# Three real products in place of four for the complex matmul of a spectral layer, inside a fused one-core Trainium2 kernel

## The chip, the cores and the metric

The kernel runs on one core of a Trainium2 chip. The metric is the device time of one launch in microseconds, taken as the median of several runs. A core has TensorE (PE: matmuls, with a queue of its own for loading the stationary operand, PEld), VectorE (DVE), ScalarE (ACT), GpSimd (POOL) and SyncE (SP, which here only starts transfers). Each engine works through its own instructions in the order of the program. Matmul results land in PSUM, from where VectorE or ScalarE must fetch them; operands lie in SBUF.

## The reference

```python
X = np.fft.rfft(x, axis=1)                       # x: (8, 3008, 256)
Xr, Xi = X.real, X.imag
Yr = Xr @ w_r - Xi @ w_i + b_r                   # w: (256, 256)
Yi = Xr @ w_i + Xi @ w_r + b_i
Yr = np.sign(Yr) * np.maximum(np.abs(Yr) - 0.01, 0.0)     # the same for Yi
y = np.fft.irfft(Yr + 1j * Yi, n=3008, axis=1)
h = y.reshape(-1, 256) @ w_in                    # w_in: (256, 2048)
g = np.where(h > 0.0, h, np.exp(np.minimum(h, 0.0)) - 1.0)
out = g @ w_out                                  # w_out: (2048, 256)
```

So each batch passes a Fourier transform along its 3008 positions, a complex matmul over 256 channels with bias and soft threshold, the inverse transform, and then a two-layer network with ELU.

## The kernel before

The transform of length 3008 = 47 x 64 is done in steps of matmuls. For each batch there are units of five kinds, named by letters:

- **A** (6 units): the first transform step. Its result goes through DRAM and comes back in another order as the tile `Z`.
- **X** (8 units, `unit_X`): the second transform step, 8 small matmuls each. Its result is `XT`, in bfloat16, with 128 channels on the partitions, two halves of channels `dt`, a plane `c` for real and imaginary parts, and 1536 frequencies. ScalarE writes it from PSUM (line 128).
- **M** (12 groups, `unit_M(b, q, i)`, written M00 to M51 here): 128 frequencies each. `m_group` sums four matmuls of 512 columns, real plane with `wcat_r` = [w_r, w_i] and imaginary plane with `wcat_s` = [-w_i, w_r], for both `dt` (line 210). VectorE adds the bias out of PSUM into `yb` (line 220). GpSimd makes `clip` and subtracts it, which is the soft threshold, into `Y` (lines 231 and 232).
- **B** (6 units): the first inverse step, two M groups each, written by ScalarE as `Bz` (line 317); again through DRAM.
- **y** (8 units): the last inverse step, which writes `yT`, the input of the network.

The network works on blocks of 512 positions with 2048 hidden values, cut into 376 slots of 256 hidden values. `front(i)` computes `hps` (line 933) in PSUM and ScalarE takes the exponential. `elu` clips it and `finish_elu` forms `gT`: on VectorE line 988 and line 977 as a rule; in a slot that holds an M group ScalarE does two steps (lines 951 and 952) and VectorE line 975 only; in a slot without any unit GpSimd clips (line 986). `back(i)` multiplies `gT` with `w_out` into `ps_o` (line 1007) two slots later, and every eighth slot `osb` is copied out (line 1019).

The order is written out by hand. While the network of batch b runs, the units of batch b+1 are put into its 47 slots by `plan(b)`, one unit a slot, in the order y, X0 to X7, M00 M01 M10 M11 B0 M20 M21 B1 and so on to B5, then A of the batch after, with the y units 6 and 7 between. In a slot the unit comes first, then the matmuls of `front`, then `gT` of the slot before, then `elu`, then the matmuls of `back`. The input transfers are started by GpSimd in three slots of a batch.

Three PSUM pools matter. All units share one tile of two banks (`psF`). `hps` has two tiles (`psH`), so the matmuls of a slot wait until `gT` of two slots earlier has read its tile. `ps_o` has two.

Batch 0 is done ahead of the network with functions of its own (`first_M`, `last_M`, which stand on `m_group` or repeat its four products); the change leaves them as they are. `last_M` (line 276) has matmuls of 256 columns.

Of the kernel before, what the change touches and what calls it, by code (L numbers as in the profile page):

```python
# [8 lines left out]
ALU = mybir.AluOpType  # L9
AF = mybir.ActivationFunctionType  # L10
BF16 = mybir.dt.bfloat16
F32 = mybir.dt.float32
# [17 lines left out]
def kernel(  # L30
# [11 lines left out]
    nc = tc.nc  # L42
    P = nc.NUM_PARTITIONS

    B, S, D = x.shape
# [5 lines left out]
    LAM = 0.01  # L51
# [9 lines left out]
    wcat_r = constp.tile([P, 2, 2 * D], BF16, name="wcat_r")  # L61
    wcat_s = constp.tile([P, 2, 2 * D], BF16, name="wcat_s")
    w_in_s = constp.tile([P, 2, DFF], BF16, name="w_in_s")
    w_out_r = constp.tile([P, NFT, E], F32R, name="w_out_r")
    bias_bc = constp.tile([P, 2 * D], F32, name="bias_bc")
# [15 lines left out]
    wk2 = ctx.enter_context(tc.tile_pool(name="wk2", bufs=2))  # L81
    wk3 = ctx.enter_context(tc.tile_pool(name="wk3", bufs=3))
# [20 lines left out]
    XT_of = {}  # L103
    Y_of = {}
# [14 lines left out]
    def unit_ps(name, alone):  # L119
        if alone:  # L120
            return pre2.tile([P, 2, 512], F32, name=name, tag="pre2")
        return psF.tile([P, 2, 512], F32, name=name, tag="fps")

    def evac(dst, src, on_dve):
        if on_dve:
            nc.vector.tensor_copy(dst, src)
        else:
            nc.scalar.copy(dst, src)  # L128
# [45 lines left out]
        q.dma_start(Z_of[b][r0:r1, s0:s1, :], dv[r0:r1, s0:s1, :])  # L174

    def unit_X(b, u, alone=False, on_dve=False, apart=False):
        g, dt = u // 2, u % 2
        if u == 0:
            XT_of[b] = xtp.tile([P, 2, 2, K1 * N2], BF16, name="XT", tag="XT")
        XT, Z = XT_of[b], Z_of[b]  # L180
        if apart:
            psv = [t[:].rearrange("p (k j) -> p k j", j=P) for t in two_banks(pre1, "mps1")]
        else:
            ps = unit_ps("xps", alone)
            psv = [ps[:].rearrange("p a (k j) -> p (a k) j", j=P)]
        nk = 8 // len(psv)
        for kk in range(8):
            k = 8 * g + kk
            nc.tensor.matmul(  # L189
                psv[kk // nk][:, kk % nk, 0 : 4 * K1], lhsT=Z[:, k, dt * P : dt * P + P],  # L190
                rhs=M2[:, k].rearrange("p c m -> p (c m)"), start=True, stop=True,
            )
        for h, v in enumerate(psv):
            k0 = 8 * g + nk * h
            evac(
                XT[:, dt].rearrange("p c (m s) -> p c m s", s=NS)[:, :, :, k0 : k0 + nk],
                v[:, :, 0 : 4 * K1].rearrange("p k (c m) -> p c m k", c=2),
                bool(h) if apart else on_dve,
            )

    mps_of = {}

    def m_group(b, q, i, ps, biased=False):
        XT = XT_of[b]
        o = (2 * q + i) * P
        todo = [(c, dt) for c in range(2) for dt in range(2)]
        if b == 0:
            todo.sort(key=lambda z: z[1])
        for c, dt in todo:
            nc.tensor.matmul(  # L210
                ps, lhsT=XT[:, dt, c, o : o + P], rhs=(wcat_r, wcat_s)[c][:, dt, :],
                start=(not biased and (c, dt) == (0, 0)), stop=((c, dt) == (1, 1)),
            )
        if i == 0:
            Y_of[b, q] = wk3.tile([P, 2, 2 * D], BF16, name="Y", tag="Y")
        if biased:
            yb = ps
        else:
            yb = wk3.tile([P, 2 * D], F32, name="yb", tag="yb")[:]
            nc.vector.tensor_tensor(yb, ps, bias_bc[:], ALU.add)  # L220
        if (b, q, i) == (0, 2, 0):
            clip = late3.tile([P, 2 * D], F32, name="gT", tag="gT")
        else:
            clip = wk2.tile([P, 2 * D], F32, name="clip", tag="clip")
        return yb, clip

    def unit_M(b, q, i):
        if i == 0:
            mps_of[b, q] = unit_ps("mps", False)
        yb, clip = m_group(b, q, i, mps_of[b, q][:, i, :])  # L230
        nc.gpsimd.tensor_scalar(clip[:], yb, LAM, -LAM, ALU.min, ALU.max)  # L231
        nc.gpsimd.tensor_tensor(Y_of[b, q][:, i, :], yb, clip[:], ALU.subtract)  # L232

    held = []

# [104 lines left out]
    def two_banks(pool, n):  # L340
        return [pool.tile([P, 512], F32, name=n, tag=n) for _ in range(2)]
# [133 lines left out]
    busy = constp.tile([P, 512], BF16, name="busy")  # L475
# [279 lines left out]
    gatep = ctx.enter_context(tc.tile_pool(name="gatep", bufs=2))  # L755
    late2 = ctx.enter_context(tc.tile_pool(name="late2", bufs=2))
    late3 = ctx.enter_context(tc.tile_pool(name="late3", bufs=3))

    w_in_v = moe_w_in.rearrange("(c p) f -> p c f", p=P)
    w_out_v = moe_w_out.rearrange("(t p) e -> p t e", p=P).bitcast(F32R)  # L760
# [23 lines left out]
    def gate(src):  # L784

        t = gatep.tile([P, 1], F32, name="gate", tag="gate")
        nc.gpsimd.tensor_copy(t[0 : src.shape[0], :], src)
# [15 lines left out]
    for u in range(8):  # L803
        unit_X(0, u, alone=True, on_dve=u == 1, apart=u > 3)
        if u == 1:
            nc.vector.tensor_tensor(w3[:], v3[:], w3[:], ALU.subtract)
        if u < 4:
            idle_pe(1)
# [88 lines left out]
    FILL = 10  # L897
# [136 lines left out]
    def put(kind, b, *a):  # L1034
        return ({"A": unit_A, "X": unit_X, "M": unit_M, "B": unit_B, "Y": unit_Y}[kind], (b, *a))

    def plan(b):

        f0 = [[] for _ in range(PER)]
        f1 = [[] for _ in range(PER)]  # L1040
        n1, n2 = b + 1, b + 2
        mid = [("X", u) for u in range(8)] + [
            ("M", 0, 0), ("M", 0, 1), ("M", 1, 0), ("M", 1, 1), ("B", 0), ("M", 2, 0),
            ("M", 2, 1), ("B", 1), ("M", 3, 0), ("M", 3, 1), ("B", 2), ("M", 4, 0),
            ("M", 4, 1), ("B", 3), ("M", 5, 0), ("M", 5, 1), ("B", 4),
            ("A", 0), ("B", 5), ("A", 1), ("A", 2), ("A", 3), ("A", 4),
        ]
        if n1 < B:
            lead, seq = 0, [("y", u) for u in range(2, 6)] + mid
            if b:  # L1050
                seq.insert(20, ("y", 6))
                seq.insert(24, ("y", 7))
                xs = (3, 8, 13)
                seq += [("A", 5)] * (5 if n2 == B else 1) + [("n", 0), ("n", 1)]
            else:
                lead, seq = FILL, (
                    [u for u in mid if u[0] != "A"]
                    + [("A", 0), ("A", 1), ("A", 2), ("n", 0), ("n", 1)]
                    + [("A", u) for u in range(3, 6)]
                )  # L1060
                xs = (12, 15, 18)
        else:
            lead, seq = 0, [("y", u) for u in range(2, 8)]
        for t, u in enumerate(seq, lead):
            if u[0] == "y":
                f0[t].append(put("Y", b, u[1]))
            elif u[0] == "n":
                f0[t].append(put("Y", n1, u[1]))
            elif u[0] == "A":
                if n2 < B:  # L1070
                    f0[t].append(put("A", n2, u[1]))
            else:
                f0[t].append(put(u[0], n1, *u[1:]))
            if u == (("A", 1) if b and n2 < B else ("B", 5)):
                f1[t] += [
                    (load_Bs, (n1, w, 0, 4 * K1 - 16 * (b == w == 0))) for w in range(4)
                ]
            if u == ("A", 5) and n2 < B:
                f1[t] += [(load_Z, (n2, s0, s1)) for s0, s1 in ((0, 8), (8, NS))]
        if b == 0:  # L1080
            for t in range(6):
                f1[t].append((unit_A, (1, t, False, t not in (0, 2), True)))
            for t, a, u in (
                (7, f0, 2), (7, f1, 3), (8, f0, 4), (8, f1, 5), (9, f0, 6), (9, f1, 7)
            ):
                a[t].append((split_Y, (0, u)))
            f1[1].insert(0, (scale_w_in, (1, True, 1)))
            for w in range(1, 4):
                f1[w].append((load_Bs, (0, w)))
            f1[5] += [(load_Z, (1, s0, s1)) for s0, s1 in ((0, 8), (8, 16), (16, NS))]  # L1090
            f1[xs[0]].append((lambda: gate(Z_of[1][:, 16, 0:1]), ()))
        if n2 < B:
            for ci in range(3):
                f1[xs[ci]].append((load_x, (n2, ci)))
        return f0, f1
# [4 lines left out]
    for i in range(n + LAG):  # L1100
        if i == FILL:
# [4 lines left out]
                        name=n_, bufs=k_, space=bass.MemoryType.PSUM, reuse_waits="tile"  # L1106
# [8 lines left out]
        elif i < n:  # L1115
            r = i % PER
            if r == 0:
                f0, f1 = plan(i // PER)
# [58 lines left out]
```

## Time and profile before

| what | value |
|---|---|
| median of 3 runs | 904.38 us (903.83 to 907.98) |
| the profiled execution | 903.61 us, span 901.8 us |
| granted TensorE clock | 0.998 |
| TensorE busy | 883.2 us (98%) |
| VectorE, ScalarE, GpSimd busy | 717.0, 696.8 and 325.5 us (80%, 77%, 36%) |
| line 210, the M groups' matmuls of 512 columns in `mps` | 342 recorded, 106.5 us busy |
| line 232, GpSimd's subtract | 84, 1276 ns each |
| line 231, GpSimd's clip | 84, 614 ns each |
| line 988, VectorE's clip of the exponential | 190, 692 ns each |

Busy time is the union of an engine's instructions. TensorE's instructions overlap each other in a pipeline, so the length of a matmul in the profile (379 ns for 512 columns) is longer than its pace, which is read from the starts of neighbours. Times in the timeline are microseconds from the start of the span; a bracket at the end of a line is the idle time before it and what ended it.

### The profile page before, as it was taken

Reading aid. Unit: us, or ns where it says so; the run is one execution under the profiler, and the core shown is the slowest. Engines: PE = TensorE matmul, PEld = TensorE weight load, DVE = VectorE, ACT = ScalarE, POOL = GpSimd, SP = SyncE. Lnnn points to the kernel's source line nnn. Section 1 sums busy time; section 2 is a strip of 40 time slices with the busy share of each in tenths; the row PEclk is TensorE's granted clock in tenths of the full one; section 3 lists DMA queues with packets and bytes.
Section 4 is the critical chain, followed back from the end, with each engine's and each line's share of the span. In section 5 each row is a group of like instructions: output and inputs, shape, how many; then the busy total and the mean of one; then the engine's idle time right before and its main releaser. Section 6 shows DMA issues by size and latency. Waiting matters only on the chain.

```text
span 901.8 us, 17335 instructions
## 1 busy us (share of the span) xinstructions
PE 883.2 (98%) x6670; PEld 653.2 (72%) x6773; DVE 717.0 (80%) x907; ACT 696.8 (77%) x876; POOL 325.5 (36%) x464
## 2 busy tenths in 40 slices
PE   8899999999999999999999999999999999999997
PEld 3467667876688667876678766787667866777776
DVE  8788768877788778897788877888778877778776
ACT  6778788877878778788887888878887877777664
POOL 7561540144230531405504153133332134443664
PEclk9999999999999999999999999999999999999999
DMA  8996226621473226713266041752228111231011
GB/s 265 308 259 188 90 68 183 199 71 48 129 200 118 71 64 163 207 60 94 59 199 187 25 110 55 213 161 81 61 73 231 28 42 50 71 96 48 24 48 48
DMA packets 90489, 105.80 MB, mean 117 GB/s; under 512 B 5363, under 2 KB 81142, under 8 KB 86982
## 3 DMA queue, kind: packets, MB, share of 16 engines
q1 hardware_dynamic: 84054, 76.64, 30.3%
q0 software_dynamic: 5968, 27.26, 9.2%
q8 instruction: 53, 0.87, 0.4%
q10 hardware_dynamic: 384, 0.79, 0.3%
q14 instruction: 30, 0.25, 0.1%
HBM read 54.86 MB, written 49.81 MB: 116 GB/s over the span
## 4 chain that ended last, share of the span: by engine, by line
PE 87%; DVE 4%; ACT 4%; issue 2%; DMA 2%; POOL 1%; DVEq 0%; SPq 0%; ACTq 0%; POOLq 0%
PE ps_o L1007 35%; PE hps L933 34%; PE mps L210 8%; PE yps L467 2%; PE bps L304 2%; PE aps L152 2%; PE xps L189 2%; DVE gT L977 1%; DVE Et L988 1%; ACT Et L954 1%; DMA xt<-in_x_dram 1%; ACT Et L951 1%; ACT Bz L317 1%; DMA Z<-DA 1%; PE sps L933 1%
## 5 line engine op out<-in xcount | busy, mean ns | idle before, releaser
L1007 PE MATMUL ps_o<-w_out_r,gT 128*128 128x256 f32 x3008 | 475.4, 301 | 0.0
L1007 PEld LDWEIGHTS ps_o<-w_out_r,gT 128*128 128x128 f32 x3008 | 403.1, 189 | 48.5 <-DVE osb L1019 1.3
L933 PE MATMUL hps<-yT,w_in_s 128*128 128x512 bf16 (+7 forms) x1613 | 372.0, 350 | 5.1
L975 DVE SCALAR_TENSOR_TENSOR gT<-Et,hps 128x512 fp32r<-128x512 f32 (+1 forms) x268 | 220.2, 851 | 73.3 <-POOL Et L986 37.0
L977 DVE SCALAR_TENSOR_TENSOR gT<-hps,Et 128x1024 fp32r<-128x1024 f32 x190 | 232.4, 1223 | 16.0 <-PE hps L933 1.4
L933 PEld LDWEIGHTS <-w_in_s 128*128 128x128 bf16 x1728 | 141.6, 98 | 128.6 <-issue 21.4
L986 POOL TENSOR_SCALAR Et<-Et 128x512 f32<-128x512 f32 x204 | 121.5, 614 | 226.8 <-ACT Et L949 217.1
L954 ACT ACTIVATE Et<-hps 128x1024 f32<-128x1024 f32 x190 | 195.7, 1030 | 9.1 <-PE hps L933 3.0
L988 DVE TENSOR_SCALAR Et<-Et 128x1024 f32<-128x1024 f32 x190 | 131.4, 692 | 44.4 <-ACT Et L954 37.4
L231 POOL TENSOR_SCALAR clip<-yb 128x512 f32<-128x512 f32 x84 | 51.6, 614 | 315.5 <-DVE yb L220 278.0
L949 ACT ACTIVATE Et<-hps 128x512 f32<-128x512 f32 x182 | 98.8, 595 | 61.9 <-PE hps L933 60.5
L951 ACT ACTIVATE Et<-hps 128x1024 f32<-128x1024 f32 x84 | 86.2, 1026 | 71.7 <-PE hps L933 70.2
L232 POOL TENSOR_TENSOR Y<-yb,clip 128x512 bf16<-128x512 f32 x84 | 107.2, 1276 | 7.0
L952 ACT ACTIVATE Et<-Et 128x1024 f32<-128x1024 f32 x84 | 88.8, 1058 | 2.7
L220 DVE TENSOR_TENSOR yb<-mps,bias_bc 128x512 f32<-128x512 f32 x88 | 60.5, 689 | 35.6 <-PE mps L210 23.4
L128 ACT CAST XT<-xps 128x768 bf16<-128x768 f32 x59 | 47.0, 799 | 14.9 <-PE xps L189 14.8
L210 PE MATMUL mps<-wcat_s,XT 128*128 128x512 bf16 x173 | 53.3, 379 | 0.8 <-issue 0.2
L210 PE MATMUL mps<-wcat_r,XT 128*128 128x512 bf16 x169 | 53.2, 384 | 0.3 <-ACT Bz L317 0.3
L128 ACT CAST A<-aps 128x1024 bf16<-128x1024 f32 x42 | 42.5, 1014 | 13.9 <-PE aps L152 12.6
L128 ACT CAST yT<-yps 128x752 bf16<-128x752 f32 x56 | 44.1, 788 | 9.2 <-PE yps L467 9.1
L210 PEld LDWEIGHTS <-XT 128*128 128x128 bf16 x380 | 30.3, 98 | 28.8 <-issue 0.9
L317 ACT CAST Bz<-bps 128x1024 bf16<-128x1024 f32 x42 | 42.0, 1000 | 1.7 <-PE bps L304 1.7
(166 smaller groups left out, 475.7 us busy)
## 6 DMA issues: line engine op xcount, KB each, us to landing
xt<-in_x_dram POOLq DMA_DIRECT2D x21, 1024.0 KB, 6.4
out_dram<-osb SPq DMA_DIRECT2D x158, 128.0 KB
Bs<-DB SPq DMA_DIRECT2D x30, 384.0 KB
DB<-Bz SPq DMA_DIRECT2D x20, 512.0 KB
DA<-A SPq DMA_DIRECT2D x19, 512.0 KB
Z<-DA SPq DMA_DIRECT2D x6, 1152.0 KB
xt<-in_x_dram POOLq DMA_DIRECT2D x6, 512.0 KB, 6.2
Z<-DA SPq DMA_DIRECT2D x8, 384.0 KB
```

Source lines behind the costliest of these rows:

```text
L128: nc.scalar.copy(dst, src)
L210: nc.tensor.matmul(ps, lhsT=XT[:, dt, c, o : o + P], rhs=(wcat_r, wcat_s)[c][:, dt, :], start=(not biased and (c, dt) == (0, 0)), stop=((c ...
L232: nc.gpsimd.tensor_tensor(Y_of[b, q][:, i, :], yb, clip[:], ALU.subtract)
L933: nc.tensor.matmul(hps[s][:, c0:c1] if early else hps[:, s, c0:c1], lhsT=w_in_s[:, dt, ft * P : ft * P + P], rhs=yT_of[b][:, dt, t0 : t0 + ...
L949: nc.scalar.activation(E_[:, s], hps[:, s], AF.Exp)
L951: nc.scalar.activation(E_, hps[:], AF.Relu, scale=-1.0)
L954: nc.scalar.activation(E_, hps[:], AF.Exp)
L975: nc.vector.scalar_tensor_tensor(o, e, -1.0, h, ALU.add, ALU.max)
L977: nc.vector.scalar_tensor_tensor(o, h, 0.0, e, ALU.max, ALU.add)
L986: nc.gpsimd.tensor_scalar(E_[s], E_[s], 1.0, 0.0, ALU.min, ALU.max)
L988: nc.vector.tensor_scalar(E_, E_, 1.0, -1.0, ALU.min, ALU.add)
L1007: nc.tensor.matmul(po[q][:, i_ % 2, :], lhsT=gT[:, s, i_ * P : i_ * P + P], rhs=w_out_r[:, ft, :], start=(ft == 0 and i_ % 2 == 0), stop=( ...
```

## The change

For batches 1 to 7 an M group is formed by three real products:

- shared = (Xr + Xi) w_r
- Yr = shared + Xi (-w_i - w_r)
- Yi = shared + Xr (w_i - w_r)

The sums of weights are made once, in place in `wcat_s`, by two GpSimd steps after batch 0 (`three_weights`). The plane Xr + Xi is made per batch by six adds of 128x512 (`sum_XT`): five on GpSimd, of which three behind X3 and two behind X7, and one on VectorE just ahead of M00. For this X is done for the first 128 channels in units 0 to 3 and for the others in units 4 to 7. An M group is then six matmuls of 256 columns, each group in a `psF` tile of its own. VectorE copies the shared product out of PSUM into one half of `yb`, then adds it to both other products. GpSimd adds the bias ahead of its clip and subtract.

```diff
     def unit_X(b, u, alone=False, on_dve=False, apart=False):
-        g, dt = u // 2, u % 2
+        g, dt = (u % 4, u // 4) if b else (u // 2, u % 2)
...
+        if b and u % 4 == 3:
+            for ch in range(dt, 3):
+                sum_XT(b, dt, ch, nc.gpsimd)
+
+    def sum_XT(b, dt, ch, eng):
+        XT, m = XT_of[b], slice(512 * ch, 512 * ch + 512)
+        eng.tensor_tensor(sum_of(dt, ch), XT[:, dt, 0, m], XT[:, dt, 1, m], ALU.add)
+
+    def sum_of(dt, ch):
+        return XS[:, 3 * dt + ch] if 3 * dt + ch < 5 else busy[:]
+
+    def three_weights():
+        r, s = wcat_r, wcat_s
+        nc.gpsimd.tensor_tensor(s[:, :, 0:D], s[:, :, 0:D], r[:, :, 0:D], ALU.subtract)
+        nc.gpsimd.tensor_tensor(
+            s[:, :, D : 2 * D], r[:, :, D : 2 * D], s[:, :, D : 2 * D], ALU.subtract
+        )
...
     def unit_M(b, q, i):
+        XT, o = XT_of[b], (2 * q + i) * P
+        if (q, i) == (0, 0):
+            sum_XT(b, 1, 0, nc.vector)
         if i == 0:
-            mps_of[b, q] = unit_ps("mps", False)
-        yb, clip = m_group(b, q, i, mps_of[b, q][:, i, :])
-        nc.gpsimd.tensor_scalar(clip[:], yb, LAM, -LAM, ALU.min, ALU.max)
-        nc.gpsimd.tensor_tensor(Y_of[b, q][:, i, :], yb, clip[:], ALU.subtract)
+            Y_of[b, q] = wk3.tile([P, 2, 2 * D], BF16, name="Y", tag="Y")
+        ps = unit_ps("mps", False)
+        ch, oc = divmod(o, 512)
+        r, s = wcat_r, wcat_s
+        for out_, lhs, w in (
+            (ps[:, 1, 0:D], None, r[:, :, 0:D]),
+            (ps[:, 0, 0:D], XT[:, :, 1, o : o + P], s[:, :, 0:D]),
+            (ps[:, 0, D : 2 * D], XT[:, :, 0, o : o + P], s[:, :, D : 2 * D]),
+        ):
+            for dt in range(2):
+                nc.tensor.matmul(
+                    out_, lhsT=lhs[:, dt] if lhs is not None else sum_of(dt, ch)[:, oc : oc + P],
+                    rhs=w[:, dt, :], start=(dt == 0), stop=(dt == 1),
+                )
+        yb = wk3.tile([P, 2 * D], F32, name="yb", tag="yb")
+        clip = wk2.tile([P, 2 * D], F32, name="clip", tag="clip")
+        evac(yb[:, D : 2 * D], ps[:, 1, 0:D], True)
+        nc.vector.tensor_tensor(
+            yb[:].rearrange("p (c d) -> p c d", c=2),
+            ps[:, 0].rearrange("p (c d) -> p c d", c=2),
+            yb[:, D : 2 * D].unsqueeze(1).to_broadcast([P, 2, D]), ALU.add,
+        )
+        nc.gpsimd.tensor_tensor(yb[:], yb[:], bias_bc[:], ALU.add)
+        nc.gpsimd.tensor_scalar(clip[:], yb[:], LAM, -LAM, ALU.min, ALU.max)
+        nc.gpsimd.tensor_tensor(Y_of[b, q][:, i, :], yb[:], clip[:], ALU.subtract)
...
+            f1[FILL + 2].append((three_weights, ()))
```

## The prediction

> **What bounds the kernel now.** I read the page's first lines, then the groups by shape, then the timeline engine by engine through one round of M and B groups, and last the timeline of the start, where VectorE and GpSimd touch each other. The page first:
>
> ```profile
> PE 883.2 (98%) x6670; PEld 653.2 (72%) x6773; DVE 717.0 (80%) x907; ACT 696.8 (77%) x876; POOL 325.5 (36%) x464
> ...
> PE 87%; DVE 4%; ACT 4%; issue 2%; DMA 2%; POOL 1%; DVEq 0%; SPq 0%; ACTq 0%; POOLq 0%
> ```
>
> TensorE is busy for 98% of the span and carries 87% of the chain that ended last. Fewer TensorE cycles should therefore pay, unless something else was only just in time. The timeline around groups B0, M20 and M21 of one batch shows how close that is. Columns are start, length, engine, line:
>
> ```profile
> 199.62 0.61 PE L210 MATMUL mps<-wcat_r,XT 128*128 128x512 bf16 x2
> ...
> 200.49 1.03 PE L933 MATMUL hps<-yT,w_in_s 128*128 128x512 bf16 x4
> ...
> 202.30 0.61 PE L210 MATMUL mps<-wcat_r,XT 128*128 128x512 bf16 x2
> ...
> 203.17 1.03 PE L933 MATMUL hps<-yT,w_in_s 128*128 128x512 bf16 x4
> ...
> 200.43 0.69 DVE L988 TENSOR_SCALAR Et<-Et 128x1024 f32<-128x1024 f32 x1 [0.60 <-ACT Et L954]
> 201.04 0.68 DVE L220 TENSOR_TENSOR yb<-mps,bias_bc 128x512 f32<-128x512 f32 x1
> 201.64 1.22 DVE L977 SCALAR_TENSOR_TENSOR gT<-hps,Et 128x1024 fp32r<-128x1024 f32 x1
> 203.45 0.69 DVE L220 TENSOR_TENSOR yb<-mps,bias_bc 128x512 f32<-128x512 f32 x1 [0.59 <-PE mps L210]
> ```
>
> The hps matmuls at 203.17 reuse the bank pair that gT of 201.64 reads until 202.86. So TensorE got the bank 0.31 us before it needed it, and VectorE (L988, yb, gT without a gap) is what fills it. In the X slots the margin is 0.17 us (gT 172.57 to 173.79, hps 173.96). TensorE is the bound with VectorE 0.2 to 0.3 us behind it.
>
> **TensorE's gain.** An M group takes from 199.62 to 200.49, 0.87 us for four matmuls of 512 columns. Matmuls of 256 columns on the same tiles stand at line 276: their five run from 43.04 to 43.60, 0.112 us each, so six take 0.67. The gain is 0.20 us a group, 84 x 0.20 = 16.8 us if TensorE stays the bound.
>
> **VectorE's additions.** yb (0.60 us to the next start) becomes a copy of 256 columns and an add of 512. The add is priced at L220. The copy has its own row, 420 ns:
>
> ```profile
> L232 POOL TENSOR_TENSOR Y<-yb,clip 128x512 bf16<-128x512 f32 x84 | 107.2, 1276 | 7.0
> ...
> L1022 DVE COPY osb<-ps_o 128x256 f32<-128x256 f32 x2 | 0.8, 420 | 0.8 <-PE ps_o L1007 0.8
> ```
>
> The add reads what the copy wrote. L988 followed by its gT shows that cost: 0.10 us after the end (208.70 + 0.69, then 209.49) where independent steps start 0.08 before it. So the pair adds 0.42 + 0.10 = 0.52 us. In the changed program only the last of the six matmuls of a group signals, and the copy waits for that one, so nothing of it is hidden under the group.
>
> M following M: from the group's start the matmuls end at 0.67, VectorE starts 0.28 later (before: 202.30 + 0.87, start 203.45), copy to 1.37, add from 1.47, gT from 2.07 to 3.29, bank free about 3.35. TensorE wants it at 2.48 + 0.67 = 3.15. It waits 0.20, and the slot stays at its 2.68 us. The three groups M01, M10, M11 gain nothing.
>
> Pairs behind a B or y slot (M20/M21 to M50/M51, four a batch): here L988 of the slot before comes late, VectorE is 0.52 longer, TensorE 2 x 0.20 earlier, and the margin was 0.31, about 0.25 after signalling. TensorE waits 0.52 + 0.40 - 0.25 = 0.67, less 0.40 gained: +0.27 a pair. Where the slot before is a y slot the margin was 0.56 (gT 221.65 to 222.87, hps 223.43), so about +0.02.
>
> **GpSimd's additions.** Each M group now has the bias add besides clip and subtract. A two-input add of 128x512 is 1.28 us (L232), clip 0.70 to the next start: 1.37 + 0.70 + 1.37 = 3.4 us a group. M, M, B takes about 7.7 us and brings 6.9 us of that, so GpSimd works nearly without pause from M00 to the last B. What this does to L988 is to be read at the start of the run, where the same kind of VectorE instruction (two SBUF sides, float32 in) meets GpSimd:
>
> ```profile
> 38.02 1.24 DVE L779 TENSOR_SCALAR w_in_s<-w_in_f 128x512 bf16<-128x512 f32 x1
> ...
> 52.87 0.42 DVE L779 TENSOR_SCALAR w_in_s<-w_in_f 128x512 bf16<-128x512 f32 x1
> ...
> 37.71 1.27 POOL L261 TENSOR_TENSOR Y<-yb,clip 128x512 bf16<-128x512 f32 x1
> ```
>
> Alone it takes 0.42. Begun under GpSimd's subtract, which ends at 38.98, it ends at 39.26, 0.28 after it: it was held until GpSimd was through. Of the 190 L988 none overlaps a GpSimd computation in the trace of before; gT and yb, which read PSUM, overlap many and keep their length. So only L988 is exposed. Met at random by a back-to-back GpSimd, it waits (1.28² + 1.28² + 0.61²) / (2 x 3.4) = 0.54 us on average and then saves 0.14 of its start: +0.39. Bounds are 0 and 1.28. That goes straight into the wait of a pair: 0.27 + 0.39 = 0.66 behind a B, 0.41 behind a y, so 2 x 0.66 + 2 x 0.41 = 2.1 us a batch.
>
> **The plane sums.** Three on GpSimd after X3, two after X7, and one on VectorE ahead of M00. I price those on GpSimd at 1.28 (bounds 0.61, the one-input row, and 1.5, the longest row of a 512 step, L714). Count from an X slot's start by the slot at 180.05: XT is written at 1.35 (181.40), L988 due 2.48 to 3.17. The sums run 1.44 to 2.72, then L988 first (it ends 3.27, GpSimd's next is held to it), 3.27 to 4.41, 4.50 to 5.78. L988 of X4, due at 4.63, is held to 5.78 and ends 6.33 in place of 5.32. One us less the margin: +0.9 a batch.
>
> M00: VectorE's sum stands in its queue behind L988 of X7, which waits for ScalarE's exp and for GpSimd's first sum; it ends at 3.27. The sum itself has no row; bounds by line 650 (96x384, 0.56) and line 806 (128x768, 0.95), I take 0.64. It ends at 3.83, TensorE at 2.15 + 0.11 = 2.26 has nothing else in its queue: a wait of 1.63, less 0.20 gained, +1.43. The page VectorE: DVE Perf Modes of the Trainium skill (the perf-mode tier table) puts a bfloat16 add from SBUF at two elements a cycle, an estimate of 0.42 here and 1.5 us less over the run; no row shows one.
>
> Nothing is moved past a queue that matters: the input DMAs of GpSimd come up to 4 us later, tens of us before their use. X1 and X2 of batch 1 read later parts of Z than before; the last part had landed by 76.40, X2 starts at 76.60. The two steps on the weights (2.6 us, once) lie beside X. B4 and B5 wait for GpSimd's last subtract, most where B5 follows B4 at once: 0 to 1 us a batch, I take 0.5.
>
> **The sum.** A batch: 0.9 + 1.43 + 0 + 2.1 + 0.5 = 4.9 us, times 7 = 34.5. The profiled execution took 903.61 (span 901.8), which gives 938.1; the median of the runs shown is 0.8 above it: 939.
>
> A rule that speaks harder against the change: the Trainium skill, SBUF — State Buffer, Who interferes with whom, has a VectorE step with two SBUF inputs blocked by a GpSimd step that reads SBUF. The row nearest is line 654, two such inputs, at 21.79: 0.60 us, no longer than its sisters, though GpSimd's L714 had begun at 21.23. So I let the DVE sum go ahead; by the rule it waits for GpSimd's second sum (see the third rival).
>
> **Rivals.**
> One, L988 isn't held: the four lines above are then four of the start only. X costs nothing, pairs 2 x 0.27 + 2 x 0.02 = 0.6, M00 3.73 - 2.26 - 0.20 = 1.3: with the B groups 0.3, 2.2 a batch, 15 in all: 919. Against it: all L779 begun under GpSimd end 0.28 after it. Chance 0.16.
>
> Two, the waits are absorbed and TensorE's gain stays, ending faster: 904 - 16.8 = 888. It decides itself at hps: VectorE's pair would have to cost under 0.10 us more than yb, not 0.52, and the M00 sum be there 1.6 us earlier. Nothing in the profile has such a cover. Chance 0.05. If only M00's wait is absorbed and L988 isn't held, the batch costs 2.2 - 1.6 = 0.6: 908, no change to be measured, chance 0.04.
>
> Three, VectorE's M00 sum is held too, by the second GpSimd sum (3.27 to 4.41), ending at 4.91: 1.1 us more a batch, 947; with GpSimd's adds at 1.5 some 953. Chance 0.2.
>
> Four, the change doesn't save TensorE time: 256 columns at line 1007's pace (1.27 us for eight, 0.158) make a group of 0.95. M00 to M11 each get 0.28 longer than I forecast, 4 x 0.28 x 7 = 8: 947. Against it stands line 276. Chance 0.04.
>
> **Numbers.** My forecast has 0.51. Eight in ten: from 917, just under the first rival, to 953. Faster by over 0.5% (4.5 us, about what a measurement of this kernel tells from no change) 0.05, within 0.04, slower 0.91.
>
> **What would show it.** Right: L988 in M and X slots longer than 0.70 with ends 0.55 behind GpSimd's; TensorE idle about 1.6 us before M00, released by DVE; idle before hps released by gT; GpSimd over 55% busy. Wrong: L988 at 0.69 beside GpSimd (first rival), or TensorE waiting for none of them and M groups of 0.67 (second).

## The result, and the profile after

The changed kernel takes 940.27 us (median of 6 runs, 938.56 to 941.77); the kernel before took 903.98 us in the same session (903.69 to 907.98). The ratio is 1.0393, with a 95% interval of 1.0373 to 1.0413: slower by 36 us. The profiled execution took 940.29 us, its span is 938.5 us and its granted clock 0.993. The forecast was 939, in a range of 917 to 953.

First the page of the changed kernel: busy times, chain, and four groups (line, engine, operation, count, then busy us, mean ns of one, and the idle time before them):

```profile
PE 883.3 (94%) x6838; PEld 673.5 (72%) x6941; DVE 776.1 (83%) x998; ACT 697.5 (74%) x876; POOL 482.3 (51%) x585
...
PE 59%; DVE 20%; ACT 11%; issue 6%; DMA 2%; POOL 1%; DVEq 0%; SPq 0%; ACTq 0%; POOLq 0%
...
L1033 DVE TENSOR_SCALAR Et<-Et 128x1024 f32<-128x1024 f32 x190 | 151.1, 795 | 44.2 <-ACT Et L999 37.7
...
L273 POOL TENSOR_TENSOR yb<-yb,bias_bc 128x512 f32<-128x512 f32 x84 | 107.6, 1281 | 78.9 <-DVE yb L268 78.7
...
L207 POOL TENSOR_TENSOR XS<-XT 128x512 bf16<-128x512 bf16 x28 | 35.2, 1272 | 126.3 <-ACT XT L128 126.3
...
L261 PE MATMUL mps<-wcat_r,XS 128*128 128x256 bf16 x140 | 31.5, 283 | 19.5 <-DVE XS L207 15.0
```

TensorE fell from 98% busy to 94%, and of the chain that ended last it now carries 59% in place of 87%; VectorE has taken 20%. Line 1033 is line 988 of before, the clip of the exponential: its mean went from 692 to 795 ns, 19.7 us more over 190 of them. The waits of TensorE name what ends them (us in total, times, longest):

```profile
PE hps L978 <- DVE gT L1022: 15.2, 46, 0.9
PE mps L261 <- DVE XS L207: 15.0, 7, 2.2
PE mps L261 <- DVE yb L268: 3.9, 12, 0.5
```

To see where the time went I laid the slots of the two traces beside each other, each from the start of its `ps_o` to that of the next. The spans differ by 36.7 us:

| slots (sum over 7 batches) | forecast | measured |
|---|---|---|
| X0 to X7 | +6.3 | +4.0 |
| M00 and M01 | +10.0 | +18.3 (17.2 and 1.1) |
| M10, M11 | 0 | -1.8 |
| the four pairs M20/M21 to M50/M51 | +14.7 | +12.5 |
| B0 to B5 | +3.5 | +4.2 (B5 2.0, B0 1.2) |
| all others | 0 | -0.4 |

**An X slot.** The timeline (start, length, engine, line) through the first three sums of the batch that follows the stretch shown of before:

```profile
187.37 1.23 DVE L1033 TENSOR_SCALAR Et<-Et 128x1024 f32<-128x1024 f32 x1
188.70 1.23 DVE L1022 SCALAR_TENSOR_TENSOR gT<-hps,Et 128x1024 fp32r<-128x1024 f32 x1
...
184.19 3.86 POOL L207 TENSOR_TENSOR XS<-XT 128x512 bf16<-128x512 bf16 x3 [15.00 <-ACT XT L128]
...
189.98 0.81 PE L978 MATMUL hps<-yT,w_in_s 128*128 128x512 bf16 x2 [0.28 <-DVE gT L1022]
```

GpSimd's three sums end at 188.05. The clip began under the third at 187.37 and ends at 188.60, 0.55 after GpSimd, and `hps` waits. This is the chain of the prediction, at the very clip that it named: 187.37 is 4.62 us behind the start of X3 at 182.75, where the prediction had 4.63.

**M00.** The same view, seven microseconds on:

```profile
194.27 0.83 DVE L1033 TENSOR_SCALAR Et<-Et 128x1024 f32<-128x1024 f32 x1
195.02 1.36 DVE L207 TENSOR_TENSOR XS<-XT 128x512 bf16<-128x512 bf16 x1
...
193.40 1.15 POOL L207 TENSOR_TENSOR XS<-XT 128x512 bf16<-128x512 bf16 x1 [4.68 <-ACT XT L128]
194.52 1.59 POOL L207 TENSOR_TENSOR busy<-XT 128x512 bf16<-128x512 bf16 x1
...
196.44 0.28 PE L261 MATMUL mps<-wcat_r,XS 128*128 128x256 bf16 x1 [2.23 <-DVE XS L207]
...
198.27 1.22 DVE L1022 SCALAR_TENSOR_TENSOR gT<-hps,Et 128x1024 fp32r<-128x1024 f32 x1
...
198.79 0.39 PE L261 MATMUL mps<-wcat_r,XS 128*128 128x256 bf16 x2
...
199.53 0.81 PE L978 MATMUL hps<-yT,w_in_s 128*128 128x512 bf16 x2
```

VectorE's sum begins at 195.02 under GpSimd's second sum, which ends at 196.11; it ends at 196.38, 0.27 later. TensorE has stood for 2.23 us when it gets it. The forecast was 1.63. The group that follows, M01, takes 0.74 us from 198.79 to `hps` at 199.53, where the four matmuls of before took 0.87; `hps` waits there for the gT that ends at 199.49. M10 has no such wait and takes 0.67 us, from 201.34 to 202.01, the very figure of the prediction.

**A pair.** M20 and M21 of the same batch:

```profile
209.58 1.24 DVE L1033 TENSOR_SCALAR Et<-Et 128x1024 f32<-128x1024 f32 x1 [0.61 <-ACT Et L999]
210.75 0.41 DVE L126 COPY yb<-mps 128x256 f32<-128x256 f32 x1
211.19 0.69 DVE L268 TENSOR_TENSOR yb<-mps,yb 128x512 f32<-128x512 f32 x1
211.80 1.22 DVE L1022 SCALAR_TENSOR_TENSOR gT<-hps,Et 128x1024 fp32r<-128x1024 f32 x1
...
209.01 1.26 POOL L273 TENSOR_TENSOR yb<-yb,bias_bc 128x512 f32<-128x512 f32 x1
...
211.94 0.39 PE L261 MATMUL mps<-wcat_r,XS 128*128 128x256 bf16 x2 [0.41 <-DVE yb L268]
...
213.06 1.02 PE L978 MATMUL hps<-yT,w_in_s 128*128 128x512 bf16 x4 [0.30 <-DVE gT L1022]
```

The bias add ends at 210.27, the clip at 210.82, again 0.55 later. The copy, the add and gT then follow without a gap, and `hps` starts as gT ends. M21's matmuls have waited too, 0.41 us for the PSUM tile that M20's add gives back at 211.88; the prediction had only the wait at `hps`.

### The profile page after: what moved, and what is told of

Same layout as the page of the kernel before. It is cut to its first block, busy times and chain, and to the rows that moved or that the text cites. A ratio compares the mean times of both kernels' runs of the same rounds, so it can differ in the third digit from the quotient of the medians.

```text
span 938.5 us, 17909 instructions
## 1 busy us (share of the span) xinstructions
PE 883.3 (94%) x6838; PEld 673.5 (72%) x6941; DVE 776.1 (83%) x998; ACT 697.5 (74%) x876; POOL 482.3 (51%) x585
## 4 chain that ended last, share of the span: by engine, by line
PE 59%; DVE 20%; ACT 11%; issue 6%; DMA 2%; POOL 1%; DVEq 0%; SPq 0%; ACTq 0%; POOLq 0%
PE hps L978 26%; PE ps_o L1052 23%; DVE gT L1022 7%; DVE Et L1033 6%; ACT Et L999 4%; ACT Et L996 3%; PE mps L261 2%; DVE yb L268 2%; ACT Bz L360 2%; PE aps L152 2%; DVE yb L126 2%; PE yps L510 2%; DVE osb L1064 1%; DVE gT L1020 1%; ACT Et L997 1%
## 5 line engine op out<-in xcount | busy, mean ns | idle before, releaser
L978 PE MATMUL hps<-yT,w_in_s 128*128 128x512 bf16 (+7 forms) x1592 | 372.6, 351 | 22.9 <-DVE gT L1022 15.2
L1033 DVE TENSOR_SCALAR Et<-Et 128x1024 f32<-128x1024 f32 x190 | 151.1, 795 | 44.2 <-ACT Et L999 37.7
L273 POOL TENSOR_TENSOR yb<-yb,bias_bc 128x512 f32<-128x512 f32 x84 | 107.6, 1281 | 78.9 <-DVE yb L268 78.7
L207 POOL TENSOR_TENSOR XS<-XT 128x512 bf16<-128x512 bf16 x28 | 35.2, 1272 | 126.3 <-ACT XT L128 126.3
L268 DVE TENSOR_TENSOR yb<-mps,yb 128x512 f32<-128x512 f32 x84 | 58.1, 692 | 2.9
L261 PE MATMUL mps<-wcat_s,XT 128*128 128x256 bf16 x336 | 51.6, 277 | 0.0
L261 PE MATMUL mps<-wcat_r,XS 128*128 128x256 bf16 x140 | 31.5, 283 | 19.5 <-DVE XS L207 15.0
```

Of the source, the lines that this page charges most:

```text
L261: nc.tensor.matmul(out_, lhsT=lhs[:, dt] if lhs is not None else sum_of(dt, ch)[:, oc : oc + P], rhs=w[:, dt, :], start=(dt == 0), stop=(d ...
L273: nc.gpsimd.tensor_tensor(yb[:], yb[:], bias_bc[:], ALU.add)
L978: nc.tensor.matmul(hps[s][:, c0:c1] if early else hps[:, s, c0:c1], lhsT=w_in_s[:, dt, ft * P : ft * P + P], rhs=yT_of[b][:, dt, t0 : t0 + ...
L1033: nc.vector.tensor_scalar(E_, E_, 1.0, -1.0, ALU.min, ALU.add)
```

## The experiments

Theory: TensorE's saving is real, but VectorE and GpSimd were so near to the path that their added steps cost more; three things add up: VectorE's longer chain, the clip held by GpSimd (it ends only when GpSimd's step is through; called the hold below), and M00 waiting for its sum. The rivals: the matmuls save nothing; the waits come from something else than the hold; M00's wait is only a matter of queue order. Ratios are to the kernel before in the same session, with 95% intervals; a cost in slots is read from one profiled execution of each kernel.

### The matmuls alone

Before, with six matmuls of 256 columns for batches 1 to 7 and the old bias add (`todo` is the list of the four matmuls of before):

```diff
+        if b:
+            for c, h, w in ((0, 0, wcat_r), (1, 0, wcat_s), (0, 1, wcat_r)):
+                for dt in range(2):
+                    nc.tensor.matmul(
+                        ps[:, D * h : D * h + D], lhsT=XT[:, dt, c, o : o + P],
+                        rhs=w[:, dt, D * h : D * h + D],
+                        start=(dt == 0 and c == 0), stop=(dt == 1 and (c, h) != (0, 0)),
+                    )
+            todo = []
```

> The kernel before, with the M groups of batches 1 to 7 as six matmuls of 256 columns and nothing else changed: VectorE takes the sum out of PSUM in one step as before, GpSimd has clip and subtract only. Left out: the plane sums and the third product in the imaginary half. Theory (TensorE's saving is real, VectorE stands 0.25 us behind it in the four pairs of a batch): in the changed kernel's trace a group takes 0.74 us against 0.87, so 0.13 to 0.20 x 84 = 11 to 17 us less, minus up to 0.15 x 28 = 4 where hps waits for gT: 888 to 895 us. Rival (256 columns save nothing, the load of the stationary tile sets the pace): 904.

Measured: 889.98 us, 0.9867 (0.9836 to 0.9898). The saving exists: 13.1 us, 0.16 a group on average where the prediction had 0.20. M00 to M11 gain about 0.21 each, as forecast, and only M21 and M51 some 0.05. That ends the fourth rival, by which 256 columns save nothing.

### VectorE's copy and add alone

```diff
-            nc.vector.tensor_tensor(yb, ps, bias_bc[:], ALU.add)
+            if b:
+                nc.vector.tensor_copy(yb[:, D : 2 * D], ps[:, 0:D])
+                nc.vector.tensor_tensor(
+                    yb.rearrange("p (c d) -> p c d", c=2),
+                    ps.rearrange("p (c d) -> p c d", c=2),
+                    yb[:, D : 2 * D].unsqueeze(1).to_broadcast([P, 2, D]), ALU.add,
+                )
+            else:
+                nc.vector.tensor_tensor(yb, ps, bias_bc[:], ALU.add)
```

> The kernel before with four products, where VectorE takes the result of an M group of batches 1 to 7 out of PSUM by a copy of 256 columns and an add of 512, as the changed kernel does. Left out: the bias (the added half is a copy of the real half instead). Theory (each pair behind a B or y slot has 0.25 us of cover and gets 0.52 more): 0.27 x 28 = 7.5 us more, 909 to 914. Rival (VectorE has idle time enough in an M slot, the copy is hidden): 904.

Measured: 908.48 us, 1.0061 (1.0046 to 1.0076), a little under the expectation. By itself the longer chain costs 5.4 us. The place is another than expected: in the profiled execution B0 to B4, whose `hps` follows the second M group, cost 4.5 us and the four pairs only 1.5.

### The bias add left out

```diff
-        nc.gpsimd.tensor_tensor(yb[:], yb[:], bias_bc[:], ALU.add)
```

> The changed kernel without GpSimd's bias add in batches 1 to 7 (left out of the result). Theory (a busy GpSimd holds L988 of the slots behind an M group, 0.39 us on average, and that goes straight into the wait of a pair): 28 x 0.39 = 11 us less, and some 3 less at the B groups: 924 to 931. Rival (the longer L988 is real but absorbed, the pairs wait for copy and add alone): 937 to 940.

Measured: 931.1 us (925.66 to 936.01), 1.0309 (1.0265 to 1.0352), at the upper end of the expectation. The pairs fell from +12.5 to +1.8 us and the 2.0 of B5 went: 12.7 us in the places where they were forecast. The clip is shorter by 68 ns on average:

```profile
L1032 DVE TENSOR_SCALAR Et<-Et 128x1024 f32<-128x1024 f32 x190 | 138.2, 727 | 44.6 <-ACT Et L998 37.9
```

But only 9 us came off the time. The rest is in M00 and M01: +22.9 there against +18.3, though TensorE's wait ahead of M00 is the same 15.0 us in all. What differs is the granted clock behind that wait, which fell to a half in six of seven batches, against three of seven with the bias add. That is the profiled execution; the others fit: 925.66 us at a granted clock of 0.995, 936.01 at 0.987.

### The clock behind M00

The changed kernel in windows of 3.41 us (length, busy time and count of PE, PEld, DVE, ACT and POOL, then the granted clock, the DMA share and GB/s); each first line is a window with a standstill ahead of M00, each second line the window after it; in the middle pair the boundary lies inside the standstill:

```profile
89.69:93.10 3.41, 1.27 (x11) 1.02 (x9) 3.41 (x4) 1.70 (x3) 2.27 (x2) 1.00 0.09 22
93.10:96.51 3.41, 3.33 (x12) 2.10 (x13) 2.03 (x4) 0.33 (x1) 0.81 (x1) 0.50 0.47 132
417.38:420.79 3.41, 2.59 (x24) 1.94 (x23) 2.94 (x5) 2.28 (x3) 1.81 (x2) 1.00 0.32 125
420.79:424.20 3.41, 2.09 (x15) 1.71 (x17) 2.56 (x4) 0.53 (x1) 1.08 (x2) 1.00 0.00 0
533.42:536.83 3.41, 1.33 (x10) 0.81 (x10) 2.47 (x4) 0.22 (x1) 1.95 (x2) 1.00 0.00 0
536.83:540.24 3.41, 3.41 (x17) 2.73 (x15) 1.88 (x3) 2.09 (x2) 2.37 (x3) 0.50 0.02 5
```

The stretches at half clock begin at 93.1, 536.8 and 649.4 us and last 3.4 us each. Their distances, 443.7 and 112.6, are 130 and 33 times 3.413: they lie on one grid, as if the chip judged fixed windows of 3.41 us. Against this grid all seven standstills of 2.07 to 2.23 us fall into place: the three that lie (nearly) whole in one window, with 2.0 to 2.1 us of it, are followed by half clock; the four that a boundary cuts, with at most 1.6 us of idle time in any one window, are not. The kernel without the bias add fits too: 1.92 us or more in one window in the six, at most 1.8 in the seventh. The Trainium skill, TensorE: Matmul & The Clock Gate (What's actually happening), describes such a free-running window of about 3.4 us, but has the clock fall after at least one idle window; here TensorE was busy for 1.3 to 1.4 us of it, and the clock fell.

To test that it is the standstill, TensorE was kept busy through the wait:

```diff
+        if (q, i) == (0, 0):
+            for _ in range(8):
+                nc.tensor.matmul(
+                    ps[:, 0], lhsT=XT[:, 0, 0, 0:P], rhs=w_in_s[:, 0, 0:512], start=True, stop=True
+                )
```

> The changed kernel with eight matmuls of 512 columns, 1.7 us, put into TensorE's queue ahead of M00; their result is overwritten. Theory (the half clock of 3.4 us that follows some of the M00 waits comes from TensorE standing still for 2.1 to 2.2 us, and costs 1.4 us each: M00 and M01 together are 3.4 to 3.6 us longer in the batches with it, 1.9 to 2.1 in those without): idle ahead of M00 0.5 us, no half clock between the first M00 and the end, 4 us less, 935 to 937. Rival (the half clock has another cause, or costs nothing): 939 to 941.

Measured: 938.65 us, 1.0382 (1.0367 to 1.0397). No half clock is left behind M00, and M00 with M01 fell from +18.3 to +13.7 us, the forecast 4.6. Yet the total moved by only 1.6 and ended between the two expectations. Two things took the rest. The pairs went from +12.5 to +14.7, and the whole 2.3 us of that lie in the three batches that had half clock before:

| the four pairs, by batch | 1 | 2 | 3 | 4 | 5 | 6 | 7 |
|---|---|---|---|---|---|---|---|
| changed kernel (half clock in 1, 5 and 6) | 1.9 | 1.9 | 2.4 | 2.5 | 1.0 | 1.5 | 1.4 |
| TensorE kept busy (no half clock) | 2.8 | 1.9 | 2.3 | 2.5 | 1.8 | 2.0 | 1.4 |

So half of what a stretch costs behind M00 comes back in the pairs of the same batch; by what, no run isolates. And the profiled execution has a half clock elsewhere: from 46.2 us on, ahead of the first slot, and the time up to the first slot is 1.75 us longer. It follows a window from 42.8 us in which TensorE is idle for 1.92 us, in pieces of at most 1.42; so the idle time need not be one standstill. The execution with a granted clock of 1.0 took 936.86 us, within the expectation. So the cause of the half clock is shown. It cost 4.6 us behind M00, of which the pairs gave 2.3 back.

### The plane sums of GpSimd left out

```diff
-            for ch in range(dt, 3):
-                sum_XT(b, dt, ch, nc.gpsimd)
```

> After without GpSimd's five plane sums a batch; VectorE's sum stays where it is, behind the clip of X7. Left out: the third product takes the real plane where a sum was made by GpSimd. If VectorE's wait ahead of M00 is the hold by GpSimd's second sum (third rival), the clip takes 0.69 and the sum 0.41 in every batch, TensorE stands about 1.1 us instead of 2.1 to 2.2, no stretch at half clock follows, and M00 with M01 go from +18.3 to +7 us; with the X slots' +4.2 gone that is 922 to 928 us. If the sum is late only because it is queued behind the clip, M00 stays at +14 to +18, only the X slots' part goes: 934 to 937 us.

Measured: 927.71 us, 1.0272 (1.0255 to 1.0289), as expected for the hold. Its M00, in the batch shown above:

```profile
191.89 0.68 DVE L1032 TENSOR_SCALAR Et<-Et 128x1024 f32<-128x1024 f32 x1
192.49 0.42 DVE L206 TENSOR_TENSOR XS<-XT 128x512 bf16<-128x512 bf16 x1
...
192.96 0.28 PE L260 MATMUL mps<-wcat_r,XS 128*128 128x256 bf16 x1 [1.23 <-DVE XS L206]
```

The same instruction takes 0.42 us where it took 1.36 beside GpSimd. TensorE stands 1.13 to 1.5 us, no half clock follows, and M00 with M01 cost +7.4. In steps: 7.4 us for the sum queued behind the clip, 13.7 - 7.4 = 6.3 for the hold by GpSimd, 4.6 for the half clock; together 18.3. The X slots fell from +4.0 to +0.4; what stays is 0.8 in X3 of the first batch, whose clip is held by GpSimd's two steps on the weights, less small gains.

### VectorE's sum one slot earlier

```diff
-        if (q, i) == (0, 0):
-            sum_XT(b, 1, 0, nc.vector)
...
+                if u == ("X", 7):
+                    f1[t].append((sum_XT, (n1, 1, 0, nc.vector)))
```

> The changed kernel with VectorE's plane sum put ahead of L988 in the slot of X7, not behind it. Theory (M00 waits because the sum is queued behind L988, which waits for ScalarE's exp and GpSimd's sum): from the start of X7 the XT tile is there at 1.35, VectorE free at 2.3, GpSimd's first sum over at about 2.6, so the sum ends near 3.0 in place of 4.6 and TensorE waits 0.8 in place of 2.5 us: 8 to 13 less, 927 to 932. Rival (M00 waits for GpSimd's sums themselves or for ScalarE's write of XT): 940, no change.

Measured: 930.52 us, 1.0306 (1.029 to 1.0321), 9.7 less, as expected. M00 with M01 fell to +7.0 and no half clock is left, while the pairs cost 14.7, as in the two kernels just shown (14.7 in both).

### Everything on GpSimd left out

The kernel with the early sum, without bias and without GpSimd's plane sums (the plane of the real part stands in their place):

> The changed kernel with all of GpSimd's additions left out (plane sums, bias) and VectorE's plane sum put ahead of L988; the products take the real plane in place of the sums that are left out. What stays is TensorE's saving, copy and add on VectorE, and one sum of 0.41 us on VectorE. Theory: minus 13 (six matmuls alone), plus 5.4 (split evacuation alone), M00 waits 0.4 us and L988 of X7 comes 0.1 later, plus 2 to 3: 896 to 901. Rival (something else in the change costs time too: the order of X units, a PSUM tile for each group): above 905.

Measured: 907.3 us, 1.005 (1.0032 to 1.0068): a miss, on the rival's side. I had added the prices of the two single parts and the early sum. The next kernel asks whether they add.

### Both together, without any work on GpSimd

The kernel before with the first two edits, to see whether their prices add:

> Before with both single parts together: six matmuls of 256 columns, and the copy of 256 columns with an add of 512 in place of the bias add. Left out: plane sums, third product in the imaginary half, bias. If the two prices add (0.9867 and 1.0061 of 903 to 904): 903.8 - 13.1 + 5.4 = 896 us, and the 907.3 of the kernel without GpSimd's work then come from its early plane sum and its tiles. If VectorE's chain (copy, add, gT) takes the place of TensorE's gain in the groups behind a B or a y slot, the pairs end near +2 in place of -6 and the whole comes to 903 to 906 us. I expect the second.

Measured: 903.91 us, 1.0012 (1.0002 to 1.0021). The two prices don't add: -13.1 and +5.4 make -7.7, and the run shows +0.7. The wait of TensorE that is longest in total (us, times, longest) says why:

```profile
PE hps L950 <- DVE gT L994: 7.5, 27, 0.3
```

With the matmuls alone the same wait is 0.3 us in all. In the pairs the copy and the add come through to `hps` as soon as TensorE is quicker, so the pairs cost +2.9 us in place of gaining; the groups M00 to M11 keep 3.2, the B slots cost 1.6. So even with nothing added on GpSimd the change would have gained nothing. The 3.4 us from here to the 907.3 of the kernel above lie in M00, which has +2.2 there and -1.5 here. There TensorE waits for VectorE's sum:

```profile
PE mps L258 <- DVE XS L206: 2.5, 7, 0.6
```

The other suspects of that miss cost nothing: with a PSUM tile for each group (the kernel above) the pairs take +2.1 us, with one for two groups (this kernel) +2.9, and the X slots in their new order take +0.3.

### Half of the bias add

The copy becomes an add of b_r (VectorE, at the same 418 ns), so that GpSimd has to add only b_i - b_r, on 256 columns; with the early sum:

```diff
-        evac(yb[:, D : 2 * D], ps[:, 1, 0:D], True)
+        nc.vector.tensor_tensor(yb[:, D : 2 * D], ps[:, 1, 0:D], bias_bc[:, 0:D], ALU.add)
...
-        nc.gpsimd.tensor_tensor(yb[:], yb[:], bias_bc[:], ALU.add)
+        nc.gpsimd.tensor_tensor(yb[:, D : 2 * D], yb[:, D : 2 * D], space[:, 0:D], ALU.add)
```

> The changed kernel with VectorE's sum ahead of L988, and half of GpSimd's bias add taken away without leaving anything out: VectorE's copy becomes an add of b_r of the same size, GpSimd adds b_i - b_r to 256 columns. Theory (what GpSimd's presence costs falls with its busy time: leaving the whole add out took 10 us off the pairs): 5 to 8 less than with the sum moved alone, 922 to 926. Rival (only a GpSimd below full occupation helps, the half add keeps it busy through the B slots): 929 to 931.

Measured: 918.86 us, 1.0164 (1.015 to 1.0178), better than expected. Half of the add took the whole hold out of the pairs (14.7 to 2.8 us, where the kernels without any work on GpSimd have 2.1 and 2.9) and out of B5. GpSimd's timeline ahead of M20's bias add shows why:

```profile
205.69 1.27 POOL L274 TENSOR_TENSOR Y<-yb,clip 128x512 bf16<-128x512 f32 x1
208.65 0.67 POOL L272 TENSOR_TENSOR yb<-yb,space 128x256 f32<-128x256 f32 x1 [1.69 <-DVE yb L267]
```

A group now costs GpSimd 2.7 us, two groups 5.4, and M, M, B lasts 7.7: it pauses for 1.69 us, and the clip of the slot ahead of the pair falls into the pause or meets only the end of a step (0.88 us at 206.63). With the whole add GpSimd's steps ran on from 203.82 to beyond 214 in the changed kernel. One cost is new: the difference of the biases is a third step beside those on the weights, and in the first batch the clips of the X slots are held the longer, one of them to 2.85 us; the X slots cost 5.8 us in place of 3.3 with the early sum alone.

### Three products only where they pay

By all this, the groups M01, M10 and M11 gain, and the pairs, in this order of the work, can't. So: before, with three products in these three groups only, two plane sums on GpSimd behind X7 (in time for M01), half bias, and weights of their own:

```diff
+        if b and u == 7:
+            for d_ in range(2):
+                nc.gpsimd.tensor_tensor(
+                    XS[:, d_], XT[:, d_, 0, 0:512], XT[:, d_, 1, 0:512], ALU.add
+                )
...
+        if (q, i) in ((0, 1), (1, 0), (1, 1)):
+            return three_M(b, q, i)
```

> The kernel before with three products in M01, M10 and M11 alone, where the next slots were 0.15 to 0.19 us shorter in the changed kernel; M00 and the groups behind a B or y slot keep four products. GpSimd makes two plane sums behind X7 and adds b_i - b_r to 256 columns, VectorE's copy adds b_r. Theory (these three have cover for copy and add, and no wait for a sum): -0.15 - 0.19 - 0.17 and +0.15 in B0, 2.5 us less in all: 899.5 to 902. Rival (GpSimd's five more steps a batch hold L988 of X7 and B0 and take it back): 903 to 906.

Measured: 901.5 us (900.68 to 902.15), before 903.81 in the same session; 0.9974 (0.9963 to 0.9985). It is 2.3 us faster than the kernel before, a small gain but one clear of the interval, and 39 us faster than the changed kernel: M01, M10 and M11 gain 3.5, B0 takes 1.2 back. The clip is at 700 ns, almost free of holds.

## Why the prediction was right, step by step

**The sum** came out at 34.5 and 36.7, the time at 939 and 940.3. That the two agree so closely is luck: M00 with M01 cost 8.3 us more than forecast, while the pairs, X, M10 with M11 and the slots put at nothing came out 6.7 lower together. The kind of the effect was right: VectorE and GpSimd take TensorE's gain back, and more. TensorE's own term was right too: a matmul group without a wait takes the 0.67 us of the prediction.

**The pairs and the hold of line 988** (14.7, measured 12.5). Without the hold the prediction had 0.6 us a batch, 4 in all: the runs show 1.8 (no bias add) to 2.9. For the hold it had 0.39 a pair, 11 in all: leaving out the bias add took 10.6 away, and between two kernels without half clock (14.7 with the whole add, 2.8 with half of it) the difference is 11.9. The first rival, that line 988 isn't held, is refuted, and the lines of the start of the run were the right evidence. The average over random meetings fitted the sum over the pairs; the single pairs are anything but alike, from -0.1 to +1.5 us. The prediction had GpSimd nearly without a pause; from the bias add of M00 to that of M51 it in fact stands idle for 7 to 11.6 of 44 to 49 us, much of it in the rounds with a y slot (some 3.6 us in each).

**M00** (10.0, measured 18.3 with M01) is the term that was mis-sized. Three things in it. The sum itself takes 0.42 and not 0.64 us, in agreement with the estimate worked out from the Trainium skill's page VectorE: DVE Perf Modes (the perf-mode tier table). That alone would have brought the term down to 8.5, beside 7.4 measured without GpSimd's sums. But the sum is held by GpSimd's second sum, which the prediction had as its third rival and set aside: in five of seven batches the sum takes 1.37 us, and in the other two the clip ahead of it is held instead (1.39 and 1.40 us). That is 6.3 us. The rule of the Trainium skill's page SBUF — State Buffer (Who interferes with whom) held here: the same sum takes 0.42 us alone and 1.37 under GpSimd's. The reading of line 654 against it doesn't stand. GpSimd's line 714, which had begun before it, takes 1.50 us, where other steps with one input of the same size take 0.61 to 0.64 (lines 231, 712 and 713), and it ends 0.34 after line 654. So there it was more likely GpSimd that was held; no run isolates it. Third, the half clock behind the standstill, 4.6 us, of which the prediction had nothing. By the third rival M00 would have cost 17.7, close to the 18.3 measured, but that too is partly luck: it had 7.7 for the hold and 0.22 a batch too much for the sum, and no half clock. Its total of 947 was not reached, because the other terms came out lower. One slip in the working: 3.83 less 2.26 is a wait of 1.57, not 1.63, which is 0.4 us over the run.

**M01, M10, M11** (0, measured +1.1, -0.9, -1.0, and -1.1 for M01 where the clock is full). The prediction let VectorE start 0.28 us after the group's matmuls and paid 0.10 between copy and add. In the trace the copy starts about 0.20 behind the matmuls (M10: 202.21, with `hps` at 202.01) and the add 0.03 to 0.04 after the copy. So gT ends early enough, and in most batches TensorE keeps 0.13 to 0.21 us of its gain a group.

**X** (6.3, measured 4.0). The mechanism is as forecast, but it costs 0.3 to 0.8 a batch (in X5 in three batches, in X6 in four) in place of 0.9: a sum takes 1.15 us and not 1.28, and GpSimd is through 0.48 us earlier after X3 than forecast (188.05 - 182.75 = 5.30, forecast 5.78). The weights' two steps, put at nothing, hold a clip once, in the first batch, and cost 0.8.

**B** (3.5, measured 4.2): B5 costs 2.0, which goes with the bias add, as forecast. B0 costs 1.2, which the prediction did not have; it stays, at 0.8 to 1.4, in every kernel here with the copy and add in M11, also with four matmuls (1.2), and is 0.1 with the six matmuls alone.

**GpSimd over 55% busy** did not come: it is 51%. The prediction's own durations add up to 51% as well (325.5 + 84 x 1.28 + 35 x 1.28 + 2.6 = 480 us of 938); the bound was not worked out from them.

**The fourth rival** read line 1007's pace as 0.158 us from the length of a row of eight; the starts of neighbours give 0.11 to 0.15. At the usual 0.142 its group would have been 0.85 us and not 0.95; the runs show 0.67.

## What to carry to other kernels

Where an engine is only 0.3 us behind the bound, a step that unloads the bound and loads that engine can gain nothing: the single prices (-13 and +5 us here) don't add, because each was taken with the other engine's work left as it was. Before a step is put on GpSimd, list the VectorE steps with two SBUF sides that run at that time, and whether GpSimd gets a pause in each round; half a step less can be worth all of it. Apply the dearer change only to the places in which no such neighbour is near, as the last experiment did.

## What the runs showed that was not expected

About 1.9 to 2.1 us of idle TensorE are enough for half clock in the next 3.41 us, if they lie in one window of a fixed grid; the same standstill cut by a boundary, with at most 1.8 us in any one window, costs nothing more. One such stretch cost about 1.5 us behind M00 (4.6 us for three), and 0.8 when what came back in the pairs is taken off. The three kernels without half clock behind M00 (TensorE kept busy, no plane sums on GpSimd, the sum one slot earlier) took between 4.6 and 11 us out of M00 and M01, and yet their pairs agree batch by batch to 0.1 us: all three differ from the changed kernel in the batches 1, 5 and 6 only. How many stretches fall behind M00 depends on where the grid lies, so the time varies from launch to launch: the six executions of the changed kernel go from 938.56 us at a granted clock of 0.997 to 941.77 at 0.992.
